# First chunk of a fused forward and backward kernel: x loaded as rows and turned on TensorE, in place of a transposing load

## The chip, the cores and the metric

The kernel runs on one core of one Trainium2 chip. The metric is the device time of one execution in microseconds, the median of several runs. The profile is of one further execution, taken by the hardware profiler. TensorE does matmuls and transposes, VectorE and ScalarE the elementwise work and the copies out of the accumulation banks (PSUM), GpSimd small copies and fills; SP (SyncE) issues most DMA transfers, and ScalarE and GpSimd a few.

## The reference

```python
# x (2,16000,256), w1 and w2 (3,256,256), g (2,8,256), w_f, w_g, w_o (256,256), all bf16
h = sum(einsum("btc,cd->btd", pad(x)[:, i:i+T], w1[i]) for i in range(3))
h = gelu(h)[:, ::2]                          # T1 = 8000
f = sum(einsum("btc,cd->btd", pad(h)[:, i:i+T1], w2[i]) for i in range(3))
f = gelu(f)[:, ::2]                          # 4000
fe, ge = f @ w_f, g @ w_g
j = tanh(fe[:, :, None, :] + ge[:, None, :, :])     # (2,4000,8,256)
out = j @ w_o
# outputs: out, and the gradients of x, w1, w2, g, w_f, w_g, w_o for a given grad_out
```

Forward and all gradients are one launch: two strided convolutions with gelu, a joint sum of 8 rows of g with every time step, tanh, a last matmul, and the way back.

## The kernel before

The 8000 output time steps (both batches in a row) are cut into 17 chunks: the first of 256, fifteen of 512, the last of 64. A chunk of 256 is laid out as 2 blocks of 128 columns, a chunk of 512 as 4 (`c.A`). Each output step stands on four steps of x.

For every chunk there are three stages. Stage a (`stage_a`) runs the convolutions: odd rows of h, even rows of h, then f and fe. They want x with its 256 channels on the partitions and time along the free axis; that layout is the tile XC, and `load_xc` fills it by transposing DMAs. GpSimd then copies XC's halo column. Stage j (`stage_j`) makes JT (tanh) on ScalarE, the output OUT_SB, the sums GWO, and the gradient with respect to the tanh's argument, with grad_out as loaded (GO) and transposed by DMA (GOT). Stage de (`stage_de`), one chunk later, makes the gradients: of f, h and x, and of w1, w2 and w_f. The gradient of w1 (`grad_w1`) multiplies x as rows, with time on the partitions (tile X, filled by `load_x`), with GHoR and GHeR, which are transposed copies of the gradients of h. A partition of X holds 4 x `c.A` + 1 rows of x and more: places 0 to 2 are the three rows ahead (the halo), the others the chunk's own. For the first chunk those are 3 + 8 rows on each of 128 partitions, and partition 0 has no halo, since time begins there: it is filled with zeros.

The order of the work is not written out by hand. `Flow` collects every operation with an engine, a cost, a due time and the buffers that it reads and writes; `issue` then plays the engines through and emits, time after time, the operation that can start first on its engine, ties by due time. So a changed cost, buffer or dependency in one chunk can change the order in all later ones. `after` and `behind` in an operation only delay its place in this plan; on the chip an instruction waits for the data and buffers that it needs and for what stands ahead of it on its engine or queue. Every engine takes its instructions in order. SP's transfers use eight semaphores in turn, so the ninth waits for the first to have landed. Buffers come in classes with a number of places: XC and X have one each, GOT three, OUT_SB three.

At the start, before the change, this stands on the engines. TensorE: 20 warm-up matmuls of 256 columns on a tile of zeros (L1047), to bring its clock up, then the odd convolution of chunk 0. SP: the transposing load of chunk 0's XC (512 KB, L361), w2, w_f, the transposing load of w_o (WOT), three loads of grad_out. ScalarE: w1, as its first instruction. GpSimd: the identity for transposes, two small loads of g (GR8), the halo copy of XC, then w_g and w_o. `make_ge` transposes g on TensorE (L1081) and multiplies it with w_g. Twelve fill matmuls (`fill`) stand on TensorE behind the first chunk's fe.

The first chunk's X for its gradients is loaded by `load_x` some 60 us into the run, in three DMAs: one row on partition 0, 15 partitions, 112 partitions (2304 elements each), and is first multiplied at 78 us.

Line numbers: matmuls are recorded at L337 (the helper `mm`), copies out of PSUM at L346 (ScalarE) and L351 (VectorE), DMAs at L361 (transposing) and L363 (plain), gelu at L514 and L517.

```python
cuts = [1, 4 * A + 1] if c.first else [1] + [4 * n + 1 for n in range(1, A + 1)]
...
dma("SP", lambda X=X: X[0:1, 3:nr], ...)                      # 1 partition
dma("SP", lambda X=X, nr=nr: X[1:16, 0:nr]..., ...)           # 15 partitions
...
dma("SP", lambda X=X, lo=lo, nr=nr: X[lo:c.Pw, 0:nr]..., ...) # lo = 16: 112 partitions
```

Of the kernel before, what the change touches and what calls it, by code (L numbers as in the profile page):

```python
# [10 lines left out]
BF16 = mybir.dt.bfloat16  # L11
FP32 = mybir.dt.float32
ALU = mybir.AluOpType
ACT = mybir.ActivationFunctionType
# [193 lines left out]
def c_pe(ns):  # L208
    return sum(max(n / 2.4 + 2.5, 25.0) for n in ns)
# [11 lines left out]
def kernel(  # L221
# [172 lines left out]
    XROWS = B * T  # L394
    st = [dict() for _ in range(NG)]

    def load_xc(k, at, behind=()):
        c = chunks[k]
        A, Pw = c.A, c.Pw
        XC = st[k]["XC"] = buf("xc", [P, 4 * NB + 1, KT, P], BF16, "XC")  # L400
        cuts = [1, 4 * A + 1] if c.first else [1] + [4 * n + 1 for n in range(1, A + 1)]
        for n, (lo, hi) in enumerate(zip(cuts, cuts[1:])):
            st[k]["XCl"] = dma("SP", lambda lo=lo, hi=hi: XC[:, lo:hi, :, :Pw].rearrange("p r k c -> p (r k) c"),
                lambda lo=lo, hi=hi: row_ap(x_, 4 * c.c0 - 1 + lo, 4 * A, Pw, hi - lo), r=[], w=[(XC, ("m", n))],
                bytes_=Pw * (hi - lo) * D * 2 * 1.3, new=[XC] if n == 0 else [], transpose=True, at=at, behind=behind, sub="xc")
        end = (XC, ("m", len(cuts) - 2))
# [50 lines left out]
    def load_x(k, at, after=()):  # L457
        c = chunks[k]
        A = c.A
        nr = 4 * A + 1  # L460
        X = buf("xc" if c.last else "x", [P, 4 * NB + 1, D], BF16, "X")
        row = 4 * c.c0 - 3
        lo, new = 0, [X]
        if c.first:
            op("POOL", 150.0, lambda e, X=X: nc.gpsimd.memset(X[0:1, 0:3], 0.0), w=[(X, "a")], new=new, at=at, after=after)
            new = []
            dma("SP", lambda X=X, nr=nr: X[0:1, 3:nr], lambda nr=nr: x[0:1, 0:nr - 3, :], r=[], w=[(X, "b")],
                bytes_=(nr - 3) * 512, at=at, after=after)
            dma("SP", lambda X=X, nr=nr: X[1:16, 0:nr].rearrange("p f d -> p (f d)"),
                lambda row=row, nr=nr: row_ap(x_, row + 4 * A, 4 * A, 15, nr), r=[], w=[(X, "c")],  # L470
                bytes_=15 * nr * 512, at=at, after=after)
            lo = 16
        rd = []
        if c.last:
# [67 lines left out]
    def stage_a(k, t0, dt):  # L542
        c = chunks[k]
        A, Pw, W = c.A, c.Pw, c.W
        S, pv = st[k], st[k - 1] if k else None
        XC = S["XC"]
        HTo = S["HTo"] = buf("hto", [P, NB + 1, KT, P], BF16, "HTo")
        G1o = S["G1o"] = buf("g1o", [P, NB + 1, KT, P], BF16, "G1o")
        HTe = buf("hte", [P, NB, KT, P], BF16, "HTe")
        G1e = S["G1e"] = buf("g1e", [P, NB, KT, P], BF16, "G1e")  # L550

        def prev(name):
            if pv is None:
# [10 lines left out]
        conv_gelu(c, [(wt(W1, i, kt), xt(2 + i, kt)) for i in range(KK) for kt in range(KT)], [(XC, ("m", n)) for n in range(1 if c.first else A)] + [W1],  # L564
                  HTo, 1, G1o, 1, [HTo])
# [12 lines left out]
        FT = buf("ft", [P, NB, KT, P], BF16, "FT")  # L578
        G2 = S["G2"] = buf("g2", [P, NB, KT, P], BF16, "G2")

        def hv(T_, lo, kt):
            return lambda: T_[:, lo:lo + A, kt, :Pw]
        taps = [(wt(W2, i, kt), hv(T_, lo, kt)) for i, T_, lo in ((2, HTo, 1), (0, HTo, 0), (1, HTe, 0)) for kt in range(KT)]
        conv_gelu(c, taps, [(HTo, 0), (HTo, 1), (HTo, "h"), (HTe, 0), (HTe, 1), W2], FT, 0, G2, 0, [FT])
        pad(c, FT)
        F.now = t0 + 0.45 * dt
        FE = S["FE"] = buf("fe", [P, NB, KT, P], BF16, "FE")
        for mt in range(KT):
            ps = psum()
# [455 lines left out]
    wps = psum()  # L1045

    def warm_up(e):  # L1047
        for _ in range(20):
            mm(wps[:, 0:2 * P], warm[:, 0, 0], warm[:, 0].rearrange("p k c -> p (k c)"), True, True)
    op("PE", 20 * 215.0, warm_up, r=[(warm, 0)], w=[wps], new=[wps])  # L1050
    op("POOL", 500.0, lambda e: make_identity(nc, ident[:]), w=[ident])
    GEB01 = []
    for b in range(B):
# [8 lines left out]
        wload(q, W2, lambda: W2[:], lambda: w2.rearrange("i (kt p) n -> p (i kt) n", p=P), 6, at)  # L1062
        wload(q, WF, lambda: WF[:], lambda: w_f.rearrange("(kt p) n -> p kt n", p=P), 2, at)

    load_xc(0, BIG)
    wload("ACT", W1, lambda: W1[:], lambda: w1.rearrange("i (kt p) n -> p (i kt) n", p=P), 6, BIG)
    for b in range(B):
        dma("POOL", lambda b=b: GR8[:, b, :], lambda b=b: g[b], r=[], w=[(GR8, b)], bytes_=4096, at=BIG, cost=550.0)
    load_w("SP", BIG + 1)
    xh = st[0]["XCl"]  # L1070
    wload("POOL", WG, lambda: WG[:], lambda: w_g.rearrange("(kt p) n -> p kt n", p=P), 2, BIG + 2, [xh])
    wload("POOL", WO, lambda: WO[:], lambda: w_o.rearrange("(kt p) n -> p kt n", p=P), 2, BIG + 3, [xh])
# [33 lines left out]
    F.now = -0.3 * W0  # L1106
    make_ge()
    GEB = GEBX = None
    if 12:
        F.now = -0.05 * W0  # L1110
        fps = psum()

        def fill(e):
            for _ in range(12):
                mm(fps[:, 0:D], WG[:, 0, 0:P], WG[:, 0], True, True)
        op("PE", c_pe([D] * 12), fill, r=[WG, (GE, 1)], w=[fps], new=[fps])
    for k in range(NG + 1):
        c = chunks[min(k, NG - 1)]
        t0, Wk = (c.t0, float(c.W)) if k < NG else (float(NP), 300.0)
# [69 lines left out]
```

## Time and profile before

| | |
|---|---|
| median of 3 runs | 786.09 us (786.05 to 786.13) |
| the profiled execution, its own time | 787.74 us |
| its span, first to last instruction | 786.0 us |
| TensorE busy | 769.5 us (98%) |
| VectorE, ScalarE, GpSimd busy | 711.4, 726.3, 93.7 us |
| DMA packets | 178.85 MB, mean 228 GB/s |
| first convolution matmul | 6.83 us |
| first matmul on X | 78.05 us |

A timeline line gives the start and the duration in us (of a merged group, from its first start to its last end), engine, line, operation, output and inputs, shape and count; in square brackets the idle time ahead of it and what released it. A plain SP or ScalarE `DMA_` row is only the issue: the data lands some us later. "PEld" is the weight load that runs beside the matmuls. The durations of single matmuls are modelled to their end and overlap; the distance of their starts is the pace. Semaphore waits stand on the instruction that waits.

### The profile page before, as it was taken

Reading aid. Unit: us, or ns where it says so; the run is one execution under the profiler, and the core shown is the slowest. Engines: PE = TensorE matmul, PEld = TensorE weight load, DVE = VectorE, ACT = ScalarE, POOL = GpSimd, SP = SyncE. Lnnn points to the kernel's source line nnn. Section 1 sums busy time; section 2 is a strip of 40 time slices with the busy share of each in tenths; the row PEclk is TensorE's granted clock in tenths of the full one; section 3 lists DMA queues with packets and bytes.
Section 4 is the critical chain, followed back from the end, with each engine's and each line's share of the span. In section 5 each row is a group of like instructions: output and inputs, shape, how many; then the busy total and the mean of one; then the engine's idle time right before and its main releaser. Section 6 shows DMA issues by size and latency. Waiting matters only on the chain. (4 is left out here: it accounts for less than half of the span.)

```text
span 786.0 us, 15627 instructions
## 1 busy us (share of the span) xinstructions
PE 769.5 (98%) x5649; PEld 534.5 (68%) x5680; DVE 711.4 (91%) x1503; ACT 726.3 (92%) x1180; POOL 93.7 (12%) x233
## 2 busy tenths in 40 slices
PE   7999999999999999999999999999999999999996
PEld 5657667576776767767677666776757767577775
DVE  5799999898998989989899898998989899899965
ACT  5999989999999999999999999999999999999833
POOL 3220110201002010020101101010020110203010
PEclk9999999999999999999999999999999999999999
DMA  9999999999999999999999999899999989989994
GB/s 187 209 206 199 250 260 229 233 250 231 222 243 228 244 232 220 240 251 220 235 220 252 224 225 238 211 255 219 225 243 217 259 212 233 237 234 241 218 207 141
DMA packets 382754, 178.85 MB, mean 228 GB/s; under 512 B 307763, under 2 KB 376469, under 8 KB 380757
## 3 DMA queue, kind: packets, MB, share of 16 engines
q1 hardware_dynamic: 381122, 176.90, 99.9%
q8 instruction: 44, 0.72, 0.4%
q10 hardware_dynamic: 1138, 0.66, 0.3%
q0 software_dynamic: 416, 0.30, 0.1%
q14 instruction: 34, 0.27, 0.1%
HBM read 51.42 MB, written 50.34 MB: 129 GB/s over the span
## 5 line engine op out<-in xcount | busy, mean ns | idle before, releaser
L653 ACT ACTIVATE JT<-FE,GE 128x512 bf16<-128x512 bf16 (+4 forms) x288 | 184.9, 693 | 0.1
L738 DVE SCALAR_TENSOR_TENSOR NGZ<-JSQ,ps 128x512 f32<-128x512 bf16 (+3 forms) x252 | 150.4, 611 | 3.1 <-PE ps L337 2.9
L337 PE MATMUL ps<-WO,JT 128*128 128x256 bf16 x1000 | 148.5, 273 | 0.0
L337 PE MATMUL ps<-GOT,WOT 128*128 128x512 bf16 (+2 forms) x544 | 146.7, 362 | 0.1
L346 ACT CAST OUT_SB<-ps 128x512 bf16<-128x512 f32 (+1 forms) x219 | 131.0, 603 | 9.6 <-PE ps L337 9.5
L725 ACT ACTIVATE JSQ<-JT 128x1024 bf16<-128x1024 bf16 (+2 forms) x129 | 130.0, 1008 | 5.6 <-DVE NGZ L738 5.2
L337 PEld LDWEIGHTS <-JT 128*128 128x128 bf16 x1000 | 97.3, 98 | 54.6 <-issue 0.5
L337 PE MATMUL GWO<-GO,JR 128*128 128x256 bf16 x1000 | 129.9, 273 | 1.4 <-ACT JR L690 0.8
L690 ACT ACTIVATE JR<-JR 128x1024 bf16<-128x1024 bf16 x112 | 120.4, 1077 | 8.1 <-DVE JR L685 7.8
L755 DVE TENSOR_TENSOR ZS<-ZS,NGZ 128x1024 f32<-128x1024 f32 (+2 forms) x102 | 115.5, 1133 | 0.4
L337 PEld LDWEIGHTS <-JR 128*128 128x128 bf16 x1000 | 97.5, 98 | 17.5 <-ACT JR L690 1.6
L520 DVE SCALAR_TENSOR_TENSOR g_s<-g_sq,ps 128x512 bf16<-128x512 bf16 (+2 forms) x102 | 65.1, 640 | 42.5 <-ACT HTo L517 35.2
L337 PEld LDWEIGHTS <-W 128*128 128x128 bf16 x612 | 58.4, 99 | 60.4 <-issue 2.8
L337 PE MATMUL ps<-XC,W 128*128 128x512 bf16 (+2 forms) x408 | 85.8, 366 | 1.3 <-DMA XC<-in_x_dram 1.3
L337 PEld LDWEIGHTS <-X 128*128 128x128 bf16 (+1 forms) x756 | 73.8, 98 | 9.7
L685 DVE TENSOR_TENSOR JR<-FER,GEB 128x1024 bf16<-128x1024 bf16 x112 | 78.0, 701 | 1.2 <-PE GWO L337 0.8
L808 DVE TENSOR_TENSOR ACC<-ACC,ps 128x512 f32<-128x512 f32 x90 | 59.4, 683 | 16.8 <-PE ps L337 16.8
L337 PEld LDWEIGHTS <-WOT 128*128 128x128 bf16 x544 | 51.4, 98 | 21.6 <-issue 0.9
L348 ACT ACTIVATE GX_SB<-ps 128x512 bf16<-128x512 f32 (+1 forms) x104 | 61.6, 620 | 2.1 <-PE ps L337 1.8
L379 POOL COPY GF<-GF 128x254 bf16<-128x254 bf16 (+1 forms) x17 | 7.4, 435 | 469.2 <-issue 312.4
L514 ACT ACTIVATE g_sq<-ps 128x512 bf16<-128x512 f32 (+2 forms) x102 | 60.6, 595 | 1.0 <-PE ps L337 0.6
L337 PE MATMUL ps<-GHoR,X 128*128 128x256 bf16 (+1 forms) x378 | 57.7, 273 | 0.0
(145 smaller groups left out, 1167.4 us busy)
## 6 DMA issues: line engine op xcount, KB each, us to landing
GO<-in_grad_out_dram SPq DMA_DIRECT2D x60, 512.0 KB, 5.2
out_dram<-OUT_SB SPq DMA_DIRECT2D x60, 512.0 KB, 6.2
X<-in_x_dram SPq DMA_DIRECT2D x15, 1088.0 KB, 7.1
out_dram<-GX_SB SPq DMA_DIRECT2D x30, 512.0 KB, 3.7
GOT<-GO SPq DMA_TRANSPOSE x65, 4.7
GO<-in_grad_out_dram SPq DMA_DIRECT2D x4, 256.0 KB, 4.9
out_dram<-OUT_SB SPq DMA_DIRECT2D x4, 256.0 KB, 3.6
XC<-in_x_dram SPq DMA_TRANSPOSE x62, 5.0
```

The lines of the kernel that those rows point to most:

```text
L337: nc.tensor.matmul(ps_ap, lhsT=lhsT, rhs=rhs, start=start, stop=stop)
L346: nc.scalar.copy(out=dst(), in_=src())
L348: nc.scalar.activation(out=dst(), in_=src(), func=ACT.Copy, scale=scale)
L514: op("ACT", c_act(W, True), lambda e, mt=mt, ps=ps: nc.scalar.activation(out=sq[:, 0:A, mt, :Pw], in_=fl(ps[:, :W], A), func=ACT.Square, s ...
L520: op("DVE", c_dve(W), lambda e, mt=mt, ps=ps: nc.vector.scalar_tensor_tensor(out=s[:, 0:A, mt, :Pw], in0=sq[:, 0:A, mt, :Pw], scalar=1.0, ...
L653: nc.scalar.activation(out=fl(jtw(JT, j)[:, mt], A)[:, :, lo:hi], in_=FE[:, 0:A, mt, lo:hi], func=ACT.Tanh, bias=GE[:, b, mt, 2 * up + j:2 ...
L685: op("DVE", c_dve(n * 2 * D, 0.5), lambda e, lo=lo, n=n, m=m, JR=JR: nc.vector.tensor_tensor(out=JR[:m, 0:n], in0=S["FER"][:m, lo:lo + n]. ...
L690: op("ACT", c_act(n * 2 * D), lambda e, n=n, m=m, JR=JR: nc.scalar.activation(out=JR[:m, 0:n], in_=JR[:m, 0:n], func=ACT.Tanh), r=[JR], w= ...
L725: nc.scalar.activation(out=JSQ[:, :, :W], in_=jtw(JT, j), func=ACT.Square)
L738: nc.vector.scalar_tensor_tensor(out=fl(zap(), A)[:, :, lo:hi], in0=fl(JSQ[:, d2, :W], A)[:, :, lo:hi], scalar=1.0, in1=fl(ps[:, :W], A)[: ...
L755: nc.vector.tensor_tensor(out=a, in0=a, in1=b, op=ALU.add)
L808: op("DVE", c_dve(512), lambda e: nc.vector.tensor_tensor(out=acc_ap().rearrange("p k d -> p (k d)"), in0=acc_ap().rearrange("p k d -> p ( ...
```

## The change

The first chunk's x is loaded once, as rows with time on the partitions, into the chunk's X tile (`first_xc`), by a plain DMA of 128 x 2048 elements that goes out first on SP. w1 follows on SP in place of ScalarE's queue. `first_columns` makes XC from X: sixteen TensorE transposes of 128x128 into PSUM, in two banks, and four copies of 128x512 by ScalarE or VectorE. The tile X stays until the gradients of the chunk; `load_x` then only adds what is missing, the zeros of partition 0 and the three halo rows of partitions 1 to 127, in one DMA of 127 x 768 elements. The 20 warm-up matmuls become 14; four matmuls on X (`stay_warm`) follow the transposes; the 12 fill matmuls become 8 and wait for fe.

```diff
+    def first_xc(at):
+        c = chunks[0]
+        nr = 4 * c.A
+        X = st[0]["X0"] = buf("x", [P, 4 * NB + 1, D], BF16, "X")
+        st[0]["XCl"] = dma("SP", lambda: X[:, 3:3 + nr].rearrange("p f d -> p (f d)"), lambda: row_ap(x_, 0, nr, P, nr),
+                           r=[], w=[(X, "m")], bytes_=P * nr * 512, new=[X], at=at)
+        return X
+
+    def first_columns(X, at):
+        c = chunks[0]
+        XC = st[0]["XC"] = buf("xc", [P, 4 * NB + 1, KT, P], BF16, "XC")
+        for g in range(c.A):
+            tr = psum(BF16)
+            for h in range(2):
+                lo = 4 * g + 2 * h
+                def trs(e, tr=tr, h=h, lo=lo):
+                    for q in range(2):
+                        for kt in range(KT):
+                            nc.tensor.transpose(out=tr[:, (4 * h + 2 * q + kt) * P:(4 * h + 2 * q + kt + 1) * P],
+                                                in_=X[:, 3 + lo + q, kt * P:(kt + 1) * P], identity=ident[:])
+                op("PE", 2 * c_pe([P] * 4), trs, r=[(X, "m"), ident], w=[(tr, h)], new=[tr] if h == 0 else [], at=at)
+            for h in range(2):
+                lo = 4 * g + 2 * h
+                evac(lambda lo=lo: XC[:, 1 + lo:3 + lo].rearrange("p r k c -> p (r k c)"), lambda tr=tr, h=h: tr[:, 512 * h:512 * h + 512],
+                     512, r=[(tr, h)], w=[(XC, ("m", 2 * g + h))], new=[XC] if g == 0 and h == 0 else [], f=0.58)
+
     def load_xc(k, at, behind=()):
...
-        cuts = [1, 4 * A + 1] if c.first else [1] + [4 * n + 1 for n in range(1, A + 1)]
+        cuts = [1] + [4 * n + 1 for n in range(1, A + 1)]
         for n, (lo, hi) in enumerate(zip(cuts, cuts[1:])):
+            if c.first:
+                break
...
     def load_x(k, at, after=()):
...
+        row = 4 * c.c0 - 3
+        if c.first:
+            X = st[0]["X0"]
+            op("POOL", 150.0, lambda e, X=X: nc.gpsimd.memset(X[0:1, 0:3], 0.0), w=[(X, "a")], at=at, after=after)
+            dma("SP", lambda X=X: X[1:P, 0:3].rearrange("p f d -> p (f d)"), lambda: row_ap(x_, 4 * A - 3, 4 * A, P - 1, 3),
+                r=[], w=[(X, "b")], bytes_=P * 1536, at=at, after=after)
+            return X
...
-        if c.first:
-            op("POOL", 150.0, lambda e, X=X: nc.gpsimd.memset(X[0:1, 0:3], 0.0), w=[(X, "a")], new=new, at=at, after=after)
-            new = []
-            dma("SP", lambda X=X, nr=nr: X[0:1, 3:nr], lambda nr=nr: x[0:1, 0:nr - 3, :], r=[], w=[(X, "b")],
-                bytes_=(nr - 3) * 512, at=at, after=after)
-            dma("SP", lambda X=X, nr=nr: X[1:16, 0:nr].rearrange("p f d -> p (f d)"),
-                lambda row=row, nr=nr: row_ap(x_, row + 4 * A, 4 * A, 15, nr), r=[], w=[(X, "c")],
-                bytes_=15 * nr * 512, at=at, after=after)
-            lo = 16
...
     def warm_up(e):
-        for _ in range(20):
+        for _ in range(14):
...
-    load_xc(0, BIG)
-    wload("ACT", W1, lambda: W1[:], lambda: w1.rearrange("i (kt p) n -> p (i kt) n", p=P), 6, BIG)
+    X0 = first_xc(BIG)
+    wload("SP", W1, lambda: W1[:], lambda: w1.rearrange("i (kt p) n -> p (i kt) n", p=P), 6, BIG)
...
     load_w("SP", BIG + 1)
+    first_columns(X0, BIG)
+    wps2 = psum()
+    def stay_warm(e):
+        for _ in range(4):
+            mm(wps2[:, 0:2 * P], X0[:, 3, 0:P], X0[:, 3], True, True)
+    op("PE", 4 * 160.0, stay_warm, r=[(X0, "m")], w=[wps2], new=[wps2], at=BIG + 1)
+    load_xc(0, BIG)
...
         def fill(e):
-            for _ in range(12):
+            for _ in range(8):
...
-        op("PE", c_pe([D] * 12), fill, r=[WG, (GE, 1)], w=[fps], new=[fps])
+        op("PE", c_pe([D] * 8), fill, r=[WG, (GE, 1), st[0]["FE"]], w=[fps], new=[fps])
```

More of the change, by code (lines that the diff above doesn't have):

```diff
@@ L399, in load_xc @@
         A, Pw = c.A, c.Pw
-        XC = st[k]["XC"] = buf("xc", [P, 4 * NB + 1, KT, P], BF16, "XC")
-        cuts = [1, 4 * A + 1] if c.first else [1] + [4 * n + 1 for n in range(1, A + 1)]
+        XC = st[k]["XC"] if c.first else buf("xc", [P, 4 * NB + 1, KT, P], BF16, "XC")
+        st[k]["XC"] = XC
+        cuts = [1] + [4 * n + 1 for n in range(1, A + 1)]
         for n, (lo, hi) in enumerate(zip(cuts, cuts[1:])):
+            if c.first:
+                break
             st[k]["XCl"] = dma("SP", lambda lo=lo, hi=hi: XC[:, lo:hi, :, :Pw].rearrange("p r k c -> p (r k) c"),
@@ L405, in load_xc @@
                 bytes_=Pw * (hi - lo) * D * 2 * 1.3, new=[XC] if n == 0 else [], transpose=True, at=at, behind=behind, sub="xc")
-        end = (XC, ("m", len(cuts) - 2))
+        end = (XC, ("m", 2 * A - 1 if c.first else A - 1))
         op("POOL", 330.0, lambda e: nc.gpsimd.tensor_copy(out=XC[:, 0, :, 1:Pw], in_=XC[:, 4 * A, :, 0:Pw - 1]),
@@ L460, in load_x @@
         nr = 4 * A + 1
+        row = 4 * c.c0 - 3
[5 more added lines that the diff above has]
+            return X
         X = buf("xc" if c.last else "x", [P, 4 * NB + 1, D], BF16, "X")
-        row = 4 * c.c0 - 3
         lo, new = 0, [X]
-        if c.first:
-            op("POOL", 150.0, lambda e, X=X: nc.gpsimd.memset(X[0:1, 0:3], 0.0), w=[(X, "a")], new=new, at=at, after=after)
-            new = []
-            dma("SP", lambda X=X, nr=nr: X[0:1, 3:nr], lambda nr=nr: x[0:1, 0:nr - 3, :], r=[], w=[(X, "b")],
-                bytes_=(nr - 3) * 512, at=at, after=after)
-            dma("SP", lambda X=X, nr=nr: X[1:16, 0:nr].rearrange("p f d -> p (f d)"),
-                lambda row=row, nr=nr: row_ap(x_, row + 4 * A, 4 * A, 15, nr), r=[], w=[(X, "c")],
-                bytes_=15 * nr * 512, at=at, after=after)
-            lo = 16
         rd = []
@@ L563, in stage_a @@
         F.now = t0
-        conv_gelu(c, [(wt(W1, i, kt), xt(2 + i, kt)) for i in range(KK) for kt in range(KT)], [(XC, ("m", n)) for n in range(1 if c.first else A)] + [W1],
+        conv_gelu(c, [(wt(W1, i, kt), xt(2 + i, kt)) for i in range(KK) for kt in range(KT)], [(XC, ("m", n)) for n in range(2 * A if c.first else A)] + [W1],
                   HTo, 1, G1o, 1, [HTo])
@@ L1047, in warm_up @@
     def warm_up(e):
-        for _ in range(20):
+        for _ in range(14):
             mm(wps[:, 0:2 * P], warm[:, 0, 0], warm[:, 0].rearrange("p k c -> p (k c)"), True, True)
-    op("PE", 20 * 215.0, warm_up, r=[(warm, 0)], w=[wps], new=[wps])
+    op("PE", 14 * 215.0, warm_up, r=[(warm, 0)], w=[wps], new=[wps])
     op("POOL", 500.0, lambda e: make_identity(nc, ident[:]), w=[ident])
@@ L1108 @@
     GEB = GEBX = None
-    if 12:
+    if 8:
         F.now = -0.05 * W0
```

## The prediction, on record before the changed kernel was run

> **What bounds the kernel now.** I read the busy shares first, then busy time by stretch, then the timeline of the start, the queue of the DMA issuer and TensorE around the first chunk's gradients, and last the trace's records of packets and landings.
>
> ```profile
> PE 769.5 (98%) x5649; PEld 534.5 (68%) x5680; DVE 711.4 (91%) x1503; ACT 726.3 (92%) x1180; POOL 93.7 (12%) x233
> ```
>
> TensorE is the bound. By stretch:
>
> ```profile
> 0.00:20.00 20.00, 15.90 (x120) 11.92 (x121) 12.01 (x39) 11.32 (x28) 6.71 (x21) 1.00 0.91 189
> 40.00:60.00 20.00, 18.23 (x137) 11.63 (x136) 19.66 (x48) 19.43 (x32) 4.92 (x11) 1.00 1.02 194
> 60.00:400.00 340.00, 338.95 (x2443) 233.89 (x2456) 320.20 (x645) 331.38 (x525) 37.56 (x88) 1.00 1.04 236
> ```
>
> Columns: stretch and length, then busy time of TensorE matmuls, weight loads, VectorE, ScalarE and GpSimd, granted clock, DMA share, GB/s. TensorE idles 4.1 us in the first 20 us, 1.8 us at 40 to 60, and 1 us in the 340 us after. So two things can move the end: work that starts earlier at the beginning, or a new TensorE stall after 60 us, which is lost whole.
>
> The start:
>
> ```profile
> 0.74 1.46 SPq L361 DMA_TRANSPOSE XC<-in_x_dram  x1
> 0.74 0.44 ACTq L363 DMA_DIRECT2D W<-in_w_dram  x1
> 1.06 4.45 PE L337 MATMUL ps<-g_sq 128*128 128x256 bf16 x20 [1.06 <-DVE g_sq L1042]
> ...
> 6.83 2.72 PE L337 MATMUL ps<-XC,W 128*128 128x256 bf16 x12 [1.32 <-DMA XC<-in_x_dram]
> ...
> 9.67 1.56 PE L337 MATMUL ps<-XC,W 128*128 128x256 bf16 x12
> ...
> 11.68 0.38 ACT L517 ACTIVATE HTe<-ps 128x256 bf16<-128x256 f32 x1
> ```
>
> The first convolution waits for the transposing load of x, 6.04 us from issue to landing. The warm-up and the first 12 matmuls start every 213 ns, the next 12 every 109 ns, from 9.88 us on: until then the clock is at half speed, although 20 warm-up matmuls ran from 1.06 to 5.3.
>
> **The start, step by step.** The row load (512 KB) goes out at 0.74. The nearest row is w1 of the kernel before, 384 KB first on an idle queue, landed 3.91 us after issue; other ends are 3.74 (grad_out, 256 KB) and 6.04 (the transposing load). I take 3.9: x lies at 4.65. w1 is now behind it on the same queue; its 768 packets of 512 bytes take 0.027 us each on 16 engines, 1.3 us, so it lands near 6. The 14 warm-up matmuls end at 1.06 + 14 x 0.213 = 4.05. Then 16 transposes of 128 columns at half clock (0.107 each) take 1.7 us, to 6.35. Their evacuations, four of 128x512, two on VectorE (0.41 by the FR copy) and two on ScalarE (0.56 by the OUT_SB casts), mostly lie beside them; the last ends near 7.0. Behind the transposes TensorE has four keep-warm matmuls (0.85 us at most) and, in the new compiled order, the four transposes of g, which were behind the first 12 convolution matmuls before. They wait for g, which GpSimd's queue landed at 7.04; with 0.26 us of their own the first convolution starts at 7.3, not 6.83. The x path alone would gain nothing.
>
> What can gain is the clock. If the denser work lifts it before 7.3, the 24 convolution matmuls take 24 x 0.109 = 2.6 us and end at 9.9, where they ended at 11.2. ScalarE's chain then carries it: it ends the second HTe at 10.95 instead of 12.06 (1.1 us), and gives a little back because two casts of GER (0.4 each) now stand ahead of FT. If the clock rises only at 9.88, 12 matmuls are slow again and the gain is 0. I take 1.0 us, ends 0 and 2 (2 with x at 4.0). Which is likelier? Count TensorE's busy time in spans of 3.41 us that end at the rise: 6.47 to 9.88 was 89% busy and lifted the clock, 3.05 to 6.47 was 66% busy and did not. Afterwards 3.05 to 6.47 has 1.0 us of warm-up and 1.8 us of transposes, 82%, between the two.
> The Trainium skill (TensorE: Matmul & The Clock Gate, Part 1) says that the clock is released after a busy window of about 3.4 us and that the window is free-running, so the phase may differ from run to run; the trace's 66% and 89% agree with it, no run here shows the phase moving, and by a moved phase the start's term is anything from 0 to 2 us.
>
> The rest of the start is covered. The six warm-up matmuls taken out lie where TensorE waits for x anyway, the four fill matmuls where it waits for JT: 0. w2 now stands behind x and w1; it landed at 8.14 and is not read before 10. WG and WO leave GpSimd's queue before its copy of XC, so earlier. grad_out and WOT move up by as much as x lands earlier, and the first GOT stands ahead of HRo and HRe; it was read at 18.31, landed at 16.64. If that cover went, each microsecond of lateness would be one of TensorE's.
>
> **The three halo rows.** Later, the load of x for the first chunk's gradients (3 + 67.5 + 504 KB in three issues) becomes one of 127 rows of 1536 bytes, 190.5 KB. A third of the bytes, but look at who carries them. In the trace's landing records the 1-row issue landed from one DMA engine, the 15-row from fifteen, the 112-row from sixteen: equal shares, a whole number of rows each. 127 is prime; equal shares over more than one engine are impossible. The likeliest reading is that **one engine carries all 127 rows**.
> The Trainium skill (DMA: Bandwidth & Descriptors, Why a DMA increments its semaphore by 16 and not by 1) states this: the engine count is the largest up to 16 that divides the outer sizes, and 127 partitions get 1. The trace agrees for 1, 15 and 112 rows; it has no 127.
>
> The price: the two 1536-byte packets in the trace took 0.065 us each; 127 x 0.065 = 8.3 us on that engine. Before, each engine had about eight packets of 4608 bytes at 0.178, 1.4 us. So one engine falls behind by 6.9 us, and what SP issues next has a sixteenth on it:
>
> ```profile
> 60.48 0.60 SPq L363 DMA_DIRECT2D GO<-in_grad_out_dram  x1
> 61.14 1.36 SPq L363 DMA_DIRECT2D X<-in_x_dram  x3
> 62.60 0.55 SPq L363 DMA_DIRECT2D out_dram<-OUT_SB  x1
> 65.77 1.57 SPq L361 DMA_TRANSPOSE HRo<-HTo  x1
> 67.43 3.54 SPq L361 DMA_TRANSPOSE GOT<-GO  x1
> 71.06 1.22 SPq L361 DMA_TRANSPOSE GHeR<-GHe  x1
> 72.34 1.25 SPq L361 DMA_TRANSPOSE GHoR<-GHo  x1
> ...
> 74.87 0.59 PE L337 MATMUL ps<-GOT,WOT 128*128 128x512 bf16 x2
> 75.31 0.59 PE L337 MATMUL ps<-FT,WF 128*128 128x512 bf16 x2
> ...
> 78.05 0.38 PE L337 MATMUL ps<-GHoR,X 128*128 128x256 bf16 x2
> ```
>
> X landed at 67.6, OUT at 68.9, HRo at 71.4, GOT at 73.1, GHeR at 73.6, GHoR at 74.8; the first matmul on X, GHoR and GHeR came at 78.05. The DMA engines were nearly idle for about 2 us of that (share 0.12 at 70 to 71, 0.54 and 0.30 at 73 to 75), which absorbs part of the lag: GHoR lands at 74.8 + 6.9 - 2 = 79.7. In the compiled order of the changed kernel two thirds of the X matmuls stand ahead of FT, right behind the GOT pair of 74.87, at 75.3. TensorE is in order, so all behind them (FT, the JT transposes, GWO, and with them ScalarE and VectorE) waits **79.7 - 75.3 = 4.4 us**. Ends: 0 (the rows spread over the engines) and 6.4 (nothing absorbed). All times here shift with the start alike, so the difference stays.
>
> **Sum.** The profiled execution took 787.74, its span 786.0 and 1.7 around it; it is 1.65 above the median of 786.09. 787.74 - 1.0 + 4.4 = 791.1, that is **789.5** against the median.
>
> The planner's order also changes through the steady chunks (x's transposes of a chunk go out in twos and ones, not in fours). TensorE idles 0.3% there, so nothing can be won; I allow 0 to 2 us of loss, taken as 0.
>
> **Rivals.** A difference of 0.2% (1.6 us) is about what a measurement of this kernel can tell from no change.
> - Forecast, 0.57: halo rows on one engine, 787.8 to 792.5 (mostly over 787.7).
> - Halo rows spread, 0.28: the shares need not be equal, and eight rows go to each of fifteen engines and seven to the last, 8 x 0.065 = 0.5 us each. For it: 190 KB instead of 574, 10 us between landing and use, and no odd row count in the trace that speaks against it. It decides from two engines on in equal parts: 4.2 us each, less the 1.4 of before and the 2 idle, leaves a lag under 1 us. Then only the start is left: 787.74 - 1.0 - 1.65 = 785.1, **faster than before**, 784.1 with the early end. It is beyond 0.2% from a start gain of 1.6 us on; I give that two thirds of this case, since of the two ends of the start's term more rows (3.74 and 3.91 us for the load) lie at the early one.
> - Cancelled, 0.08: GHoR is late, but the first matmul on it waits as late as in the old order (78.05), a stall of 1.65; or the clock rises only at 9.88 and nothing stalls. 786.1 to 786.8.
> - A steady stall, 0.07: the split loads of x arrive late in the later chunks, 788 or more, whatever the halo does. Against it: XC landed at 91.9 and was read at 93.7, so there is slack.
>
> So faster 0.28 x 2/3 = 0.19, slower 0.57 and 0.07 less a little, 0.63, and within 0.2% the remaining 0.18. The range runs from the second case's early part to the forecast's late end, 784.3 to 792.3.
>
> **What would show it.** Right: the 127-row load takes over 9 us to land, GHoR over 5 us (2.5 before), and a TensorE idle of some 4 us stands ahead of the first matmul on X, released by a DMA; the 24 first matmuls at 109 ns, the second HTe near 11. Wrong: the load lands in 4 to 5 us and TensorE goes through 75 us without a gap; or the first convolution starts before 6.5, so that the start is worth more than 2 us.

## The result and the profile after

| | before | changed |
|---|---|---|
| median of 4 runs | 786.11 us (786.05 to 786.43) | 796.42 us (794.65 to 798.96) |
| ratio | | 1.0125, interval 1.0108 to 1.0142 |
| the profiled execution: time, span | 787.74, 786.0 us | 794.65, 792.6 us |

The change costs 10.3 us, where 3.4 were forecast. The profiled execution of the changed kernel lies 1.8 us below its median, and that of before lay 1.65 above its own: what the two profiles show side by side is 6.6 us of span, not 10.3. The other microseconds have to be found among the runs.

The same views as before, of the changed kernel. First the engines, then the stretches:

```profile
PE 770.2 (97%) x5657; PEld 534.1 (67%) x5690; DVE 718.0 (91%) x1522; ACT 720.7 (91%) x1165; POOL 87.7 (11%) x233
```

```profile
0.00:20.00 20.00, 15.86 (x134) 12.12 (x135) 13.60 (x44) 13.58 (x34) 9.03 (x25) 1.00 0.89 190
40.00:60.00 20.00, 17.73 (x135) 11.39 (x134) 19.55 (x49) 19.43 (x31) 4.18 (x11) 1.00 0.98 195
60.00:400.00 340.00, 335.07 (x2414) 230.88 (x2425) 318.24 (x638) 326.78 (x511) 29.09 (x86) 1.00 1.04 232
400.00:740.00 340.00, 335.15 (x2451) 233.14 (x2467) 316.05 (x653) 317.78 (x501) 39.50 (x91) 1.00 1.01 228
```

The last of these stretches in the profile of before:

```profile
400.00:740.00 340.00, 338.06 (x2478) 235.44 (x2491) 314.74 (x643) 326.27 (x515) 36.52 (x89) 1.00 1.02 230
```

TensorE's first 20 us are as before. From 60 to 740 us it idles 9.8 us (3.0 before), and not in one place: 4.9 in each half. VectorE has 6.6 us more work than before and ScalarE 5.6 less.

The timeline of the start:

```profile
0.74 0.40 SPq L363 DMA_DIRECT2D X<-in_x_dram  x1
1.20 1.01 SPq L363 DMA_DIRECT2D W<-in_w_dram  x2
4.31 1.61 PE L417 MATMUL psb<-ident,X 128*128 128x128 bf16 x16
6.58 0.42 DVE L351 COPY XC<-psb 128x512 bf16<-128x512 bf16 x1 [0.15 <-ACT XC L346]
7.43 0.20 PE L1117 MATMUL psb<-ident,GR 8*128 8x8 bf16 x2 [0.94 <-DMA GR<-in_g_dram]
10.80 0.39 ACT L545 ACTIVATE HTe<-ps 128x256 bf16<-128x256 f32 x1
```

x lands at 4.3, the last columns are copied at 7.0, the transposes of g hold TensorE until 7.5, and the second HTe starts at 10.80, 0.9 us earlier than in the profile of before. So far as forecast.

SP's queue and TensorE around the gradients of the first chunk:

```profile
60.26 0.52 SPq L363 DMA_DIRECT2D X<-in_x_dram  x1
60.89 4.42 SPq L363 DMA_DIRECT2D out_dram<-OUT_SB  x1
66.16 5.68 SPq L361 DMA_TRANSPOSE HRo<-HTo  x1
71.94 3.06 SPq L361 DMA_TRANSPOSE GOT<-GO  x1
75.09 1.22 SPq L361 DMA_TRANSPOSE GHeR<-GHe  x1
76.43 1.20 SPq L361 DMA_TRANSPOSE GHoR<-GHo  x1
```

```profile
75.28 0.59 PE L337 MATMUL ps<-GOT,WOT 128*128 128x512 bf16 x2
78.98 0.38 PE L337 MATMUL ps<-GHoR,X 128*128 128x256 bf16 x2 [3.11 <-DMA GHoR<-GHo]
```

Behind the load of 127 rows the next issue takes 4.42 us (0.55 before) and the one after it 5.68 (1.57 before): SP itself is held up. GHoR goes out at 76.43, 4.1 us later than before, and TensorE waits for it at the place that the new order gives to X. The trace's packet records say who carries the rows: 127 packets of 1536 bytes, 0.065 us each, that start one behind the other, every 0.062 us, from 64.23 to 72.08. The landing was recorded at 72.47, 12.2 us after the issue.

TensorE's waits from 400 to 740 us; the columns are total us, number and longest:

```profile
PE ps L337 <- DVE g_s L548: 3.3, 6, 0.8
PE ps L337 <- ACT OUT_SB L346: 0.2, 1, 0.2
PE ps L337 <- ACT FT L545: 0.2, 1, 0.2
```

In the profile of before the waits for g_s from 60 to 740 us sum to 0.2:

```profile
PE ps L337 <- DVE g_s L520: 0.2, 1, 0.2
```

Busy time counts each matmul to its modelled end, beside the next one, and misses a record here and there, so I made an account that depends on neither: each matmul record is put to its place in the program, and TensorE's idle time is the time that passed less the matmuls' own pace at full clock (0.109 us for 256 columns), so that half speed counts as idle too. Us of idle time by stretch, from the profiled executions:

| | 0 to 60 | 60 to 100 | 100 to 250 | 250 to 740 | to the end | sum |
|---|---|---|---|---|---|---|
| before, profile on record | 12.1 | 0.7 | 0.7 | 2.7 | 3.5 | 19.8 |
| changed | 12.3 | 4.1 | 0.1 | 7.4 | 3.1 | 27.1 |

Two things were lost: 3.4 us around the halo load and 4.7 us in the chunks from 250 us on, where the code is unchanged but for the order. The start gained nothing by 60 us.

### The profile page after: what moved, and what is told of

It is laid out like the page before. It is cut to its first block, busy times and chain, and to the rows that moved or that the text cites. A ratio compares the mean times of both kernels' runs of the same rounds, so it can differ in the third digit from the quotient of the medians.

```text
span 792.6 us, 15604 instructions
## 1 busy us (share of the span) xinstructions
PE 770.2 (97%) x5657; PEld 534.1 (67%) x5690; DVE 718.0 (91%) x1522; ACT 720.7 (91%) x1165; POOL 87.7 (11%) x233
## 4 chain that ended last, share of the span: by engine, by line
PE 58%; ACT 17%; DVE 16%; DMA 4%; issue 4%; POOL 0%; DVEq 0%; ACTq 0%; POOLq 0%; SPq 0%
PE ps L337 48%; PE GWO L337 9%; DVE g_s L548 4%; ACT JT L681 4%; DVE NGZ L766 3%; ACT JSQ L753 3%; ACT JR L718 2%; ACT g_sq L542 2%; ACT OUT_SB L346 2%; DMA GOT<-GO 2%; DVE g_sq L561 2%; PE psb L521 1%; DVE ZS L783 1%; ACT HTo L545 1%; ACT g_s L557 1%
## 5 line engine op out<-in xcount | busy, mean ns | idle before, releaser
L681 ACT ACTIVATE JT<-FE,GE 128x512 bf16<-128x512 bf16 (+4 forms) x288 | 178.7, 684 | 0.0
L337 PE MATMUL ps<-GOT,WOT 128*128 128x512 bf16 (+2 forms) x544 | 144.6, 362 | 4.5 <-DVE g_s L548 1.9
L337 PE MATMUL ps<-WO,JT 128*128 128x256 bf16 x1000 | 145.2, 273 | 0.1
L753 ACT ACTIVATE JSQ<-JT 128x1024 bf16<-128x1024 bf16 (+2 forms) x121 | 122.4, 1013 | 14.8 <-DVE ZS L766 7.4
L346 ACT CAST OUT_SB<-ps 128x512 bf16<-128x512 f32 (+1 forms) x209 | 122.2, 597 | 8.5 <-PE ps L337 8.4
L557 ACT ACTIVATE g_s<-g_s 128x1024 bf16<-128x1024 bf16 (+2 forms) x51 | 51.4, 1010 | 15.7 <-DVE g_s L548 15.6
L542 ACT ACTIVATE g_sq<-ps 128x512 bf16<-128x512 f32 (+2 forms) x102 | 59.0, 579 | 2.1 <-PE ps L337 1.9
```

The lines of the kernel that those rows point to most:

```text
L337: nc.tensor.matmul(ps_ap, lhsT=lhsT, rhs=rhs, start=start, stop=stop)
L346: nc.scalar.copy(out=dst(), in_=src())
L542: op("ACT", c_act(W, True), lambda e, mt=mt, ps=ps: nc.scalar.activation(out=sq[:, 0:A, mt, :Pw], in_=fl(ps[:, :W], A), func=ACT.Square, s ...
L681: nc.scalar.activation(out=fl(jtw(JT, j)[:, mt], A)[:, :, lo:hi], in_=FE[:, 0:A, mt, lo:hi], func=ACT.Tanh, bias=GE[:, b, mt, 2 * up + j:2 ...
L753: nc.scalar.activation(out=JSQ[:, :, :W], in_=jtw(JT, j), func=ACT.Square)
```

## The experiments

The theory (A): the halo load costs by the wait that it causes, and more in runs in which the clock drops; the order that the planner makes of the later chunks costs by itself; the start is worth about nothing. Its rivals: the halo is the whole loss and the later waits follow from it (B); the start costs (F); what is lost is the split of x's transposing loads, or an engine that got more work.

### The start alone, in the old order

A kernel can be made to follow a list of (operation, engine) in place of the planner's choice. The list here is the plan of before, with the changed kernel's start ahead of it; the halo rows go as 15 and 112 rows.

```diff
-            best = None
-            for e, lst in avail.items():
+            best = self.listed(T, lanes, nlane) if self.order else None
+            for e, lst in avail.items() if best is None else ():
```

> The changed kernel with the halo rows as 15 and 112 rows, and with the planner's choice replaced by a list: up to the columns of the first chunk the order of the changed kernel, from there on the order and the choice of engines of the kernel before, operation by operation. TensorE, ScalarE, VectorE, GpSimd and SP run the same instructions in the same order as in the kernel before, but for the start and the halo load. Theory A (what was left of the loss, 3.7 us in the kernel with split halo and fours, is the order of the later chunks): 785 to 786.6, and the lag to the kernel before stays constant from 20 us to the end. Rival F (the new start itself costs): 788 to 790, and the lag is there by 60 us. Rival G (holding x in its buffer from the start, and loading it in another way, costs in the later chunks): over 787, with a lag that grows after 100 us.

Measured: 786.43 us against 786.53, ratio 0.9998, interval 0.9989 to 1.0006. No worth of the whole start with its transposes can be seen (the interval reaches from 0.9 us faster to 0.5 slower), and nothing else is lost in this kernel: the account has 10.4, 1.3, 0.1, 2.6 and 3.8. Its stretches read like those of before:

```profile
60.00:400.00 340.00, 338.60 (x2442) 233.65 (x2454) 320.20 (x642) 331.38 (x525) 37.53 (x88) 1.00 1.03 235
400.00:740.00 340.00, 338.21 (x2475) 235.24 (x2489) 314.88 (x644) 326.31 (x517) 36.54 (x89) 1.00 1.03 232
```

F is out. But the account of before's profile starts with 12.1, this one with 10.4; why are the times the same?

> The kernel before, unchanged, profiled once more. Its runs here fell into two groups, about 784 and 785.8 us of span. Theory: the groups differ in when the clock rises in the start; in the profile on record it rose at 9.88 us, in the kernel before with the 127-row load, whose start is the same, at 6.25. So this profile, if its span is near 784, shows the rise before 8 us and the 24 first convolution matmuls at 109 ns, and if its span is near 786 it shows the rise at 9 us or later. Rival: the groups come from elsewhere, and the rise does not go with the span.

Measured: 786.08 us, span 784.3, and the start of this second profile of the unchanged kernel:

```profile
1.06 4.36 PE L337 MATMUL ps<-g_sq 128*128 128x256 bf16 x20 [1.06 <-DVE g_sq L1042]
6.62 1.47 PE L337 MATMUL ps<-XC,W 128*128 128x256 bf16 x12 [1.20 <-DMA XC<-in_x_dram]
8.21 1.48 PE L337 MATMUL ps<-XC,W 128*128 128x256 bf16 x12
10.14 0.39 ACT L517 ACTIVATE HTe<-ps 128x256 bf16<-128x256 f32 x1
```

All 24 first matmuls run at 0.109 us: the clock rose at 5.20 us, not at 9.88. The second HTe starts at 10.14, earlier than in the changed kernel. Its account is 10.6 up to 60 us and 18.2 in all. Matmul by matmul this profile is 1.55 us ahead of the one on record, from 20 us on and still at the end, so the two differ in the start alone. The time of the rise varies from run to run, and the profile on record was of an unlucky run.

### The halo rows

The changed kernel with the 127 rows in two DMAs, everything else in its place:

```diff
-            dma("SP", lambda X=X: X[1:P, 0:3]..., lambda: row_ap(x_, 4 * A - 3, 4 * A, P - 1, 3), ...)
...
+                for lo, hi in ((1, 16), (16, P)):
+                    nc.sync.dma_start(out=X[lo:hi, 0:3]..., in_=row_ap(x_, 4 * A * lo - 3, 4 * A, hi - lo, 3))
```

> The changed kernel, its 127 halo rows loaded as 15 rows and 112 rows; every other instruction of every engine stands where it stands in the changed kernel. Theory A (two costs: the halo load stalls TensorE for 3.5 us and drops its clock in most runs, and the new order of the later chunks costs 3.5 us by itself): the gap of 3.1 us ahead of the first matmul on X is gone, the two halo loads land in under 4 us each, every run has a granted clock of 0.998 or more, and the time is 789.5 to 791.5; TensorE still waits for g_s (L548) at 400 to 600 us as in the changed kernel. Rival B (the halo load is the whole loss, the later stalls follow from it): 786 to 787.5, and the waits for g_s at 400 to 600 us go as well. Rival C (the halo costs only the gap that the profile shows, and the lost clock has another cause): 792.5 to 793.5, mean clocks from 0.992 to 0.999 as before.

Measured: 791.15 us, ratio 1.0064, interval 1.0043 to 1.0086, three clocks of 0.999 and one of 0.997. SP's queue, with the halo as two issues in one row:

```profile
60.00 1.07 SPq L498 DMA_DIRECT2D X<-in_x_dram  x2
61.19 0.54 SPq L363 DMA_DIRECT2D out_dram<-OUT_SB  x1
64.80 1.51 SPq L361 DMA_TRANSPOSE HRo<-HTo  x1
66.40 3.21 SPq L361 DMA_TRANSPOSE GOT<-GO  x1
```

```profile
73.91 0.59 PE L337 MATMUL ps<-GOT,WOT 128*128 128x512 bf16 x2
74.34 0.38 PE L337 MATMUL ps<-GHoR,X 128*128 128x256 bf16 x2
```

The long issues are gone and X is used at 74.34 without a wait. The 127 packets now start between 62.75 and 65.20; the two loads took 5.5 and 5.0 us to land, not under 4. The account: 0.7 at 60 to 100, as before, and still 7.3 at 250 to 740, with the same waits for g_s. So A stands (789.5 to 791.5); B and C are out.

The other way round, the kernel before with one load of 127 rows among three, in its own order:

```diff
-            dma("SP", lambda X=X, nr=nr: X[0:1, 3:nr], ...)
-            dma("SP", lambda X=X, nr=nr: X[1:16, 0:nr]..., ...)
-            dma("SP", lambda X=X, lo=lo, nr=nr: X[lo:c.Pw, 0:nr]..., ...)
+            dma("SP", lambda X=X, nr=nr: X[0:64, 3:nr]..., ...)
+            dma("SP", lambda X=X: X[1:P, 0:3]..., ...)
+            dma("SP", lambda X=X, nr=nr: X[64:P, 3:nr]..., ...)
```

> The kernel before, with its three loads of X (1, 15 and 112 rows) exchanged for three that hold the 127-row halo: 64 rows of 4096 bytes, 127 rows of 1536, 64 rows of 4096. The order on every engine is that of the kernel before; nothing of the start is changed. Theory A: the one engine that carries 127 rows lags some 7 us, GHoR lands some 4 us later than 74.8, and the first matmul on X, at 78.05 in this order, waits 0.5 to 2 us; 786.6 to 788.5, or up to 3 us more where the gap lowers the clock. Rival E (the halo load alone does no harm, it needs the order of the changed kernel, which uses X earlier): 785.9 to 786.4, no gap.

Measured: 790.62 us, ratio 1.0048, interval 1.0030 to 1.0066: the halo load alone, no other part of the change. (The two loads beside it have 64 rows of 3072 bytes by the packets, not 4096.) E is out. X is used late in this order and TensorE still waits, longer than the 0.5 to 2 us expected:

```profile
77.12 0.62 PE L494 MATMUL psb<-ident,FE 128*128 128x128 bf16 x8
80.28 0.38 PE L337 MATMUL ps<-GHoR,X 128*128 128x256 bf16 x2 [2.54 <-DMA GHoR<-GHo]
```

```profile
80.00:100.00 20.00, 19.72 (x133) 13.48 (x133) 16.67 (x35) 16.80 (x26) 2.87 (x8) 0.91 0.96 230
```

Behind the wait the granted clock is 0.91 over 20 us: half speed for 3.41 us, from 81.34 to 84.75. That is the second part of the price; the account has 4.5 us at 60 to 100, where before has 0.7. (Another such stretch, from 43.79, lies ahead of the load and cannot come from it; the last section tells where it lies. Three of the four runs have a mean clock of 0.994 or 0.995, as this profile with its two stretches, so a part of the 4.5 us between the medians is not shown to be the load's.)

The changed kernel with its 127 rows, in the old order:

> The changed kernel, 127-row halo load and all, with the order of the kernel before from the first chunk's columns on. Theory A: only the halo's cost is left, as in the kernel before with the 127-row load (790.6): 789 to 792, a gap of 1.5 to 3 us ahead of the first matmul on X, clocks between 0.992 and 0.999. Rival (the halo hurts only where the order is the new one): 785 to 787.

Measured: 792.13 us, ratio 1.0064, interval 1.0048 to 1.0081; clocks 0.994 and 0.995. The wait ahead of X is only 0.75 us; the larger one came later, for a GOT that SP had issued late (at 87.74, in the kernel with the rows split at 79.88), and half speed behind it again:

```profile
94.48 1.64 PE L431 MATMUL ps<-GOT,WOT 128*128 128x512 bf16 x4 [2.70 <-DMA GOT<-GO]
```

The place was not the one expected, the price was, within 0.1 us. Here too a stretch of half speed, from 43.55, lies ahead of the load.

Is the lower clock a result of the wait? The changed kernel again, with 30 matmuls on constant weights in front of the first matmul on X, into the accumulator which that matmul clears:

```diff
+                if ACC is ACC1 and c.first and not held:
+                    held.append(key)
+                    for _ in range(30):
+                        mm(ps[:, 0:D], WG[:, 0, 0:P], WG[:, 0], True, True)
```

> The changed kernel with 30 matmuls on constant weights (30 x 0.109 = 3.3 us) put in front of the first matmul on X, into the accumulator that this matmul then clears; they fill the 3.5 us in which TensorE waits for GHoR, and change the order of nothing else. Theory (the wait's price is its length plus half-speed windows that it triggers; the mean clocks of 0.992 to 0.997 come from it): the wait is filled but not shortened, all runs have a clock of 0.998 or more, and the median falls from 796.4 to 794 to 795.2. Rival (the lost clock comes from other idle times, at 20 to 60 us, or has no place): clocks still from 0.992 to 0.999, 796 to 797. Rival (filling hides nothing, the matmuls come on top): 798 or more.

Measured: 796.03 us (795.23 to 797.31). Right in the clocks, 0.998 to 1.000 where the changed kernel had 0.992 to 0.999, and the spread halves. Wrong in the time: the median falls by 0.4 us, which is not resolved and lies in the range of the rival. So four runs of each kernel speak for the wait as the source of the lost clock, but it makes the spread of the runs more than their median; where the clock fell in the runs that were not profiled is not on record.

### The order

The start and the three loads of before, in the order and with the engines of the changed kernel's plan:

> The kernel before, its start and its three loads of X as they were, with the planner's choice replaced by the order and the choice of engines of the changed kernel (the split transposing loads of x in twos and ones among it). Nothing else of the change is in it. Theory A: the order costs 3.5 to 5 us by itself: 789.5 to 791, clock 0.998 or more, TensorE waits for g_s (L521 in this kernel's numbering) at 400 to 760 us, lag growing from 300 us on. Rival B (the order costs only behind the changed start or the halo's stall): 786 to 787.

Measured: 791.29 us, ratio 1.0055, interval 1.0040 to 1.0070, 0.3 above A's range; account 7.3 at 250 to 740. (The list stands ahead of the code, so the line of g_s is L620 here.) Not one instruction of the change's own is in this kernel, and it loses about half of what the change lost.

What in the order? The fill's new wait for fe is what makes the planner load x in twos and ones. Without it, x is loaded in fours again; first with the 127 rows, then with 15 and 112:

```diff
-        op("PE", c_pe([D] * 8), fill, r=[WG, (GE, 1), st[0]["FE"]], w=[fps], new=[fps])
+        op("PE", c_pe([D] * 8), fill, r=[WG, (GE, 1)], w=[fps], new=[fps])
```

> The changed kernel, its eight fill matmuls no longer made to depend on FE, as it was in the kernel before. With that the planner puts the transposing loads of x of a chunk into fours again, as before, instead of twos and ones; the 127-row load stays. Theory A: the steady order's 3.5 us come back and the halo's cost stays: 790 to 793.5, clocks between 0.992 and 0.999, no sum of waits for g_s over 1 us at 400 to 600 us. Rival B (halo is everything): unchanged, 795 to 797. Rival D (the order is everything, the halo's stall is made good later by TensorE): 786 to 787.5.

> Both of the above together: halo rows as 15 and 112 rows, fill without the dependency on FE. What is left of the change is its start: x as rows, transposed on TensorE, w1 on the same queue, 14 warm-up matmuls. Theory A: both costs are gone, 785.5 to 787.5, clock 0.998 or more. Rival (the start itself costs, for instance through the convolution's wait for g): 788 or more. Rival (the start's earlier clock is a gain of 1 us or more, as predicted): under 785.3.

Measured: 794.16 us (ratio 1.0095, interval 1.0066 to 1.0125) and 789.81 us (1.0039, 1.0024 to 1.0054). The medians differ by 4.4 us, but both of A's ranges are missed. The first time lies 0.7 us above its 793.5. The second lies 2.3 above its 787.5, in the range of the rival that the start costs, which the start in the old order has ruled out. The second kernel has 5.5 us of idle time at 250 to 740, where before has 2.7 and the one with the same halo rows and x in twos and ones has 7.3. So most of the order's loss is not in the split of x's loads: 1.8 of 4.6 us went with it, in one profile each.

Is every other plan as dear? The kernel before, with one number changed that only the planner reads:

```diff
-        op("PE", c_pe([D] * 12), fill, r=[WG, (GE, 1)], w=[fps], new=[fps])
+        op("PE", c_pe([D] * 24), fill, r=[WG, (GE, 1)], w=[fps], new=[fps])
```

> The kernel before with one number that only the planner reads: the fill of 12 matmuls is announced as 24. The same instructions run, the loads of x stay in fours, the order of a part of the rest comes out otherwise. Theory H (the order of the kernel before is a lucky or chosen one, and most other plans cost some us, whatever moved them): 787.5 to 791. Rival (the cost belongs to the orders with split or later transposing loads of x): 785.5 to 787.

Measured: 787.27 us (ten runs, 785.84 to 789.84), ratio 1.0016, interval 1.0003 to 1.0029; the profiled run, one of the fastest with 785.99, has an account of 3.1 at 250 to 740. The median lies between H and its rival, and five of the ten runs lie in H's range. So another plan need not cost 4.8 us, but that most plans cost something is not excluded.

The two plans also differ in the engine of 124 operations, most of them copies out of the accumulators (one of the 124 is the load of w1, which stayed on ScalarE's queue here). The new order with the old engines, and the old order with the new ones:

> The kernel before in the order of the changed kernel (791.3 as such), but each of the 124 operations for which the two plans choose another of ScalarE and VectorE goes to the engine of the kernel before. Theory J (TensorE's waits for g_s come from accumulator evacuations that moved to VectorE, 718 us busy instead of 711): the waits for g_s go, 787 to 788.5. Rival K (it is the order in which TensorE and SP are fed): 790 to 792. Rival (order and engines belong together): over 792.

> The kernel before in its own order, but those 124 operations on the engine that the changed kernel's plan chose. Theory J: 788.5 to 791, with waits of TensorE for VectorE. Rival K: 785.8 to 787.3. Rival (order and engines belong together): over 792.

Measured: 807.49 us (ratio 1.0274, interval 1.0252 to 1.0295) and 801.38 us (1.0192, 1.0176 to 1.0207). J and K both fall; the third case is the one that came. A plan's order and its engines belong together. In the first mixture TensorE waits for VectorE in the same place, only longer:

```profile
PE ps L437 <- DVE g_s L620: 10.3, 10, 1.6
```

Last, the place itself. In the new order TensorE asks for two or more accumulators right behind the second convolution, and the matmuls into GWO, which has a bank of its own, stand behind them; before they stand ahead. In five chunks that group was put ahead:

```diff
 second convolution, last HTe
+GWO<-GO,JR x8
 GOT,WOT x2 (W1T,GHe x2 or GOT,WOT x2 and WO,JT x4)
-GWO<-GO,JR x8
 FT,WF x4
```

> The kernel before in the order of the changed kernel, with five groups of eight matmuls moved: in the five chunks from 490 to 690 us, the GWO<-GO,JR group that stands one to three groups behind the last HTe matmuls of the second convolution is put right behind them. These eight matmuls add into GWO's own bank and need no new accumulator, and the kernel before has them in that place. Every other engine's order is unchanged. Theory L (TensorE waits for g_s because the new order asks for two more accumulators right there, while the seven that there are wait for the gelu chain): the five waits of 0.5 to 0.8 us for g_s go, and the time falls by 2 to 4 us against the same order without the move, to 787.5 to 789.5. Rival M (the engines' chain is the limit there; the wait only moves to FT or the next accumulator): less than 1 us, 790.3 to 791.8, and the waits are found a few matmuls later.

> The kernel before in the order of the changed kernel once more, as what the kernel with the moved groups is compared with on the same chip: 790.5 to 792, with the waits of TensorE for g_s at 400 to 760 us.

Measured: 790.40 us (ratio 1.0060, interval 1.0039 to 1.0080) against 791.93 (1.0065, 1.0053 to 1.0077): the intervals overlap. TensorE at the place, first the new order, then with the group moved:

```profile
494.80 0.59 PE L437 MATMUL ps<-GOT,WOT 128*128 128x512 bf16 x2
496.05 0.59 PE L437 MATMUL ps<-W1T,GHe 128*128 128x512 bf16 x2 [0.65 <-DVE g_s L620]
496.48 0.38 PE L437 MATMUL ps<-W1T,GHo 128*128 128x256 bf16 x2
496.69 1.04 PE L437 MATMUL GWO<-GO,JR 128*128 128x256 bf16 x8
```

```profile
495.77 1.04 PE L437 MATMUL GWO<-GO,JR 128*128 128x256 bf16 x8
496.64 0.59 PE L437 MATMUL ps<-GOT,WOT 128*128 128x512 bf16 x2
497.07 0.59 PE L437 MATMUL ps<-W1T,GHe 128*128 128x512 bf16 x2
...
501.03 0.71 PE L437 MATMUL ps<-GFR,HRe 128*128 128x256 bf16 x5 [0.24 <-DVE NGZ L838]
```

The waits for g_s at 400 to 740 us went from 3.3 us to 0.2. The idle time at 490 to 700 us went only from 3.9 to 3.2: in each of the five chunks three or four gaps of 0.1 to 0.4 us took the place of one of 0.7 to 1.0, at the matmuls on FT, the transposes of FT and the next accumulators. L gave 2 to 4 us, M less than 1. The medians, 1.5 us apart, decide for neither; the idle time of the two profiles says M. The wait that the profile names was where the chain of ScalarE and VectorE became visible, not what set its length. What in the order of these two engines makes the chain longer stays open.

## Why the prediction was wrong

The direction was right, and so was the engine that carries the halo rows; the size was not, 10.3 us against 3.4.

- **One engine carries the 127 rows**: right. 8.3 us of packets were predicted; they took from 64.23 to 72.14, and the load was 12.2 us under way (over 9 predicted). The Trainium skill (DMA: Bandwidth & Descriptors, Why a DMA increments its semaphore by 16 and not by 1) gives 127 partitions one engine; the 127 packets that start one at a time agree, and 15 and 112 rows overlap.
- **The stall ahead of X, 4.4 us (0 to 6.4)**: right in place and kind, 3.3 us from the end of the matmuls before it to 78.98 in the profile. GHoR landed at 78.85 (79.7 predicted). How it became late was put wrongly: its own landing took 2.4 us, not over 5; SP could not issue it in time, because its two issues ahead were held for 4.42 and 5.68 us. In four pairs of kernels, with the 127 rows and without, the medians lie 4.4 to 5.7 us apart. Not all of that is shown to be the halo's. The two of a pair run the same matmuls in the same order, so one profile can be set against the other, matmul by matmul: from 58 us, when the load has not gone out yet, to 250 us the lag grows by 2.9 us (changed kernel), 3.2 (kernel before, against its second profile), 4.3 (old order) and 2.4 (loads in fours). Another 1.3 to 3.9 us of lag was there by 58 us; in three of the four a stretch of half speed, from 18.38, 43.55 or 43.79, is most of it. What the halo itself costs is thus 2.4 to 4.3 us by the profiles, near the 4.4 of the sum.
- **The steady order, taken as 0, at most 2**: this is the step that failed. The new plan, its order with its engines, costs 4.8 us by itself (before_neworder, where the order is all that differs from before). The reason given, that TensorE idles only 0.3% there, bounds a gain and says nothing of a loss. The row that could have warned of one stood in the first line of the page: VectorE at 91% and ScalarE at 92% beside TensorE at 98%. The rival "a steady stall" named the right stretch with 0.07, but by the wrong cause, late loads of x, and no sum had it together with the halo. Which instructions of the order make the loss stays open.
- **The start, -1.0**: the profile shows most of it (the second HTe ends at 11.19, predicted 10.95, before 12.06), the median does not (ratio 0.9998). The gain was that of the earlier clock, and the second profile of before, whose 786.08 us are the median's, has that already. The 1.65 us between the profiled run and the median, which the sum took off at its end, was the same early clock. It was counted twice.
- **The clock behind the stall**: not in the sum at all. The single runs of the changed kernel lie 4.3 us apart, and the slower they are, the lower is their mean clock (0.999 at 794.65 us, 0.992 at 798.96).

Put together from the runs: 786.1 + 0 for the start + 4.8 for the order + the halo load. With the 4.4 to 5.7 us of the medians that is 795.3 to 796.6, and the median is 796.4; with the 2.4 to 4.3 of the profiles it is 793.3 to 795.2, and the profiled run, which has no half speed behind the wait, took 794.65.

## What to carry to other kernels

When a planner decides the order, a change in one place is a change of the whole plan: compare the orders first, and where three engines are over 90% busy, give the new order a price of its own with both signs. Cutting a load down to the few rows that are missing can cost more than loading all of them: look at how many rows there are, and not at the bytes. Before you correct from the profiled run to the median, ask in what these runs differ; it may be the very thing that your change improves.

## What the runs showed of the hardware

Once the clock has risen, half speed comes in stretches of 3.41 us or twice that (the last one, cut off by the end, left out), and the first rise of the clock came anywhere from 4.0 to 10.0 us in 16 profiles. Count windows of 3.413 us from that rise and take TensorE's busy share in each, every matmul at its own pace (the shares are good to some 3 points). The windows ahead of a first rise were 72% busy or more; 66% did not lift the clock. The transposes count in this: in three profiles of the changed start the window ahead of the rise held 42 to 57% of matmuls and 34 to 49% of transposes. Of the later windows at full speed (the last 12 us left out), the seven that were followed by half speed were 16 to 37% busy, and of those that were not only one lay as low as 37%. The changed kernel's stall of 3.3 us fell on the border of two windows in the profiled run, which left them 57% and 47% busy, and the clock stayed; in the kernel before with 127 rows the wait left one window 31% busy, and the clock fell. So a wait of this size can cost its own length, or up to 1.7 us more (half of 3.41), by where it falls. The kernel before has such a place of its own: around 40 us TensorE is thinly used, in the two profiles of before a window there was 43 and 47% busy, and in three others, where the windows fell otherwise, it was 29 to 35% and half speed followed at 43.6 to 45.0.

The Trainium skill (TensorE: Matmul & The Clock Gate, Part 1) says that the window is free-running and 3413 ns long, and the traces agree with both. The Trainium skill's advice to allow no idle gap above about 3 us (TensorE: Matmul & The Clock Gate, Why this matters for your kernels) is too generous here: a single wait of 2.5 us was enough in the kernel before with 127 rows, and in the loads in fours several gaps that left 2.15 us of idle time within one window.

A DMA that a single engine carries holds up the queue that issued it: SP stood 4.4 and 5.7 us at two later, unrelated issues, although from 68.8 to 73.6 us all engines together moved only 22 to 35 GB/s, where 232 is the mean from 60 to 400 us. All five profiles with the 127-row load show such long issues; with 15 and 112 rows they are gone.

Moving 123 of some 4200 planned operations between ScalarE and VectorE, with no change of order, cost 15 us: with three engines this full, the balance is part of the order.
